# The second matmul of the first MoE: one float32 product in place of three rounded ones

## The chip, the core and the metric

The kernel runs on one core of a Trainium2 chip. The metric is the device time of one execution in microseconds; of the kernel before there are three runs, with a median of 643.16 us (642.65 to 646.45). One more execution was taken with the hardware profiler; every reading below is of that one. The engines are TensorE (PE, with its weight loads, PEld), VectorE (DVE), ScalarE (ACT), GpSimd (POOL) and SyncE (SP, which issues most of the DMAs).

## The reference

Three layers follow each other, all in float32 from outside:

```
# 1. state-space attention: 4 x 8 heads, 768 tokens, chunks of 32
y = (C B^T * decay) x + C state * decay          -> x of 3072 tokens x 256
# 2. first MoE (one dense expert)
h = x @ w_in            # 3072x256 @ 256x2048
g = h * cos(h)
x = g @ w_out           # 3072x2048 @ 2048x256
# 3. second MoE: 8 experts, the best one for each token, capacity 768
e = argmax(x @ w_gate); h = relu(x @ w1[e]); out = gate * (h @ w2[e])
```

The expert of a token is an argmax, so the first two layers are computed to nearly full float32.

## The kernel before

The 3072 tokens are six tiles of 512. For each tile the first MoE runs over 16 blocks f of 128 of the 2048 hidden features: 96 iterations, `it = 16 t + f`. One iteration is

- `mm1` (L919): six matmuls of 128x128 weights by 512 tokens into one PSUM bank `hp` (three banks rotate). Weights and tokens are split into a rounded high and a low part of the type F32R, and three of the four products are taken, for two halves of the 256 inputs;
- the cosine: `c_round` (ACT, L926), `c_frac` (DVE, L930), `c_sin` (ACT, L933), `c_mul` (DVE, L936), which leaves `g = h cos(h)` in float32 in a buffer `g` (three rotate) and frees `hp`;
- `c_hi`: the high part `gh` of g, by DVE (L947), or by ACT (L945) in the iterations 3 to 15 and 79 to 93; `c_lo`: the low part `gl = g - gh` by POOL (L952). Each has three buffers;
- `mm2` (L964): six matmuls of the type F32R, the products high x high, low x high and high x low for two halves of the 256 outputs, added up in two PSUM banks `yt` over the 16 blocks.

The weights come as 64-bit words of which the kernel puts together float32 numbers: `w_c1`, `w_c2`, `w_c3` (DVE, L879, L884, L889), once for each f, for w_in and w_out at a time (`wcv`, 512 columns). `w_hi` (ACT, L901) and `w_lo` (POOL, for some blocks DVE, L905) then split each half into its parts. This happens during the prologue and the first tile.

In the same stretches the other layers run: attention for the tiles that follow (`a_s`, L781; `a_m`, DVE L789, which multiplies scores in PSUM into `ex`; `a_y`, L835 and L839; `a_diff`, a POOL operation on 128x2048, L670), the routing of the tile before (`r_evac` to `r_store`, lines 970 to 1110; DVE L978 takes `yt` out of PSUM), and the conversion of the second MoE's weights (`w2_units`, DVE L1250). After the 96 iterations the second MoE works through 58 jobs of 128 tokens by half an expert (`b_mm1` L1606, `b_mm2` L1631, L1635). Its transposed activations `ht` use the buffers of `gh` and `gl` again, and its `hr` those of `g`.

The order on all engines is one list, written out by hand: every step is put at a position (its iteration number plus an offset from the table `OFF`, in iterations, with variants for the first tiles and the last one), the list is sorted, and each engine works off its own steps strictly in that order. So mm2 of iteration `it` is put at it + 4.08, behind mm1 of iteration it + 4:

```
for _, _, fn, a in sorted(work, key=lambda w: w[:2]):
    fn(*a)
```

Of the kernel before, what the change touches and what calls it, by code (L numbers as in the profile page):

```python
# [12 lines left out]
I32 = mybir.dt.int32
I64 = mybir.dt.int64
U32 = mybir.dt.uint32
AF = mybir.ActivationFunctionType
ALU = mybir.AluOpType
# [79 lines left out]
 'gh': 1.4743,
 'gh@0': 1.227,
 'gh@5': 1.853,
 'gl': 2.061,  # L100
 'gl@0': 1.372,
 'gl@5': 2.675,
# [249 lines left out]
 'woh': -2.85,
 'woh@2': -15.528,
 'woh@3': -5.859,
 'woh@4': -2.895,
 'wol': -2.362,
 'wol@2': -12.533,
 'wol@3': -3.479,
 'wol@4': -2.851,
# [15 lines left out]
def fused_kernel(ctx: ExitStack, tc: tile.TileContext, I, out: bass.AP):  # L375
    nc = tc.nc
    P = 128
    B, H, S = 4, 8, 768
    NTOK = B * S
    D = 256  # L380
    NCH = NTOK // P
    CPB = S // P
    T = 512
    NT = NTOK // T
    CT = T // P
    NF = 16
# [121 lines left out]
    C = {}  # L508
# [362 lines left out]
    WCV = {}  # L871

    def w_words(f):
        st = WST[f]
        return st.rearrange("p a b -> p (a b)").bitcast(I32).rearrange("p (a b) -> p a b", b=2)
# [9 lines left out]
                                       op0=ALU.logical_shift_right, op1=ALU.bitwise_or)  # L885

    def w_c3(f):
        a = WCV[f]
        nc.vector.scalar_tensor_tensor(a, w_words(f)[:, :, 1], -1073741824, a,  # L889
                                       op0=ALU.bitwise_and, op1=ALU.bitwise_or)  # L890
        WST.pop(f)

    def w_part(f, which, part):
        a = WCV[f].bitcast(F32)[:, which * D:(which + 1) * D]
        if which == 0:
            return a, w_in[:, f, part].rearrange("p k c -> p (k c)")
        return a, w_out[:, f, part, :]

    def w_hi(f, which):
        a, hi = w_part(f, which, 0)  # L900
        nc.scalar.activation(hi, a, AF.Copy)  # L901

    def w_lo(f, which, eng):
        a, hi = w_part(f, which, 0)
        eng.tensor_tensor(w_part(f, which, 1)[1], a, hi.bitcast(F32), op=ALU.subtract)  # L905
# [29 lines left out]
    def c_mul(it):  # L935
        nc.vector.tensor_tensor(GT[it], HP.pop(it), GT[it], op=ALU.mult)  # L936

    GHA = [[3, 16], [79, 94]]
    gh_act = lambda it: any(a <= it < b for a, b in GHA)

    def c_hi(it):
        gh = mq.tile([P, T], F32R, tag="gh", name="gh", bufs=3)
        GH[it] = gh
        if gh_act(it):
            nc.scalar.activation(gh, GT[it], AF.Copy)  # L945
        else:
            nc.vector.tensor_scalar(gh, GT[it], 1.0, None, op0=ALU.mult)  # L947

    def c_lo(it):
        gl = mq.tile([P, T], F32R, tag="gl", name="gl", bufs=3)  # L950
        GL[it] = gl
        nc.gpsimd.tensor_tensor(gl, GT.pop(it), GH[it].bitcast(F32), op=ALU.subtract)  # L952

    def mm2(it):
        t, f = divmod(it, NF)
        if f == 0:
            YT[t] = [ps.tile([P, T], F32, tag=f"yt{k}", name="yt") for k in range(2)]
        gh, gl = GH.pop(it), GL.pop(it)
        terms = [(j, k) for j in range(3) for k in range(2)]
        if f == NF - 1:  # L960
            terms.sort(key=lambda x: x[1])
        for j, k in terms:
            wl, g = ((0, gh), (1, gh), (0, gl))[j]
            nc.tensor.matmul(YT[t][k], w_out[:, f, wl, k * P:(k + 1) * P], g,  # L964
                             start=(f == 0 and j == 0), stop=(f == NF - 1 and j == 2))
# [302 lines left out]
    V, GP = nc.vector, nc.gpsimd  # L1268
    work = []

    def put(name, pos, fn, *a, t=None):
# [79 lines left out]
        (w_hi, 0, 0),
        (w_hi, 0, 1),
        (w_lo, 0, 0, GP),
        (w_lo, 0, 1, GP),
# [14 lines left out]
        (w_hi, 1, 0),
        (w_hi, 1, 1),  # L1370
        (w_lo, 1, 0, GP),
        (w_lo, 1, 1, GP),
# [9 lines left out]
        (a_st, 1, 1),  # L1382
    ]
    for n, (fn, *a) in enumerate(prologue):
        put(f'p{n}', .1 * n - 20, fn, *a)


    for it in range(NIT):
        t, f = divmod(it, NF)
        put('mm1', it, mm1, it, t=t)  # L1390
        put('rnd', it, c_round, it, t=t)
        put('frc', it, c_frac, it, t=t)
        put('sin', it, c_sin, it, t=t)
        put('mul', it, c_mul, it, t=t)
        put('gh', it, c_hi, it, t=t)
        put('gl', it, c_lo, it, t=t)
        put('mm2' if f else 'mm2f', it, mm2, it, t=t)
    for f in range(NF):
        if f > 3:
            put('wld', f, w_load, f, t=f)  # L1400
        for k, fn in enumerate((w_c1, w_c2, w_c3)):
            if f > 1:
                put(f'wc{k + 1}', f, fn, f, t=f)
        if f > 1:
            put('wih', f, w_hi, f, 0, t=f)
            put('woh', f, w_hi, f, 1, t=f)
            put('wil', f, w_lo, f, 0, GP, t=f)
            put('wol', f, w_lo, f, 1, V if f in [2, 11, 12, 13] else GP, t=f)
# [122 lines left out]
    part = lambda i: (0, i) if i < NE else (1, i - NE)  # L1531
    XK, XR, HT, YA = {}, {}, {}, {}
# [57 lines left out]
    HPB, HR, YP, SC = {}, {}, {}, {}  # L1590
# [211 lines left out]
```

## Time and profile before

| | us |
|---|---|
| three runs, median | 643.16 (642.65 to 646.45) |
| the profiled execution, its time | 644.14 |
| its span, first to last instruction | 642.4 |
| PE busy | 546.6 |
| DVE busy | 524.4 |
| POOL busy | 388.3 |
| ACT busy | 336.9 |
| mean granted TensorE clock | 0.932 of full speed |

The program is read in stages. Until about 33 us there is the prologue. From 33 to 105 us the iterations 0 to 11 run while the weights are put together; from there until about 446 us the remaining iterations run, with attention until about 366 us; after 453 us only routing, weights and the second MoE are left. A busy PE includes the time in which a matmul that stands alone drains, and matmuls at a lower clock take longer, so that a PE that is busy is not yet a PE at its peak. In the timeline, the distance between the starts of two rows is what a group of matmuls cost in the stream.

### The profile page before, as it was taken

To read this page: it belongs to the slowest core of one execution; us is meant where nothing else is said; L and a number is where in the kernel's file an instruction comes from. 1 tells how busy PE (TensorE), PEld (TensorE's weight loads), DVE (VectorE), ACT (ScalarE), POOL (GpSimd) and SP (SyncE) were. 2 spreads that over 40 slices of the span, in tenths; PEclk is the share of its full clock that TensorE was granted. 3 is DMA by queue.
4 is the path that set the end of the run, shared out by engine and by line. 5 is a ranking of instruction groups with operands and counts; after the bars stand their busy time and mean duration, and the time that the engine had idled before them with its cause. 6 is when DMAs were issued, how large, how long until landed. Compare 5 with 4: busy or idle time off the path is not lost. (4 is left out here: it accounts for less than half of the span.)

```text
span 642.4 us, 9919 instructions
## 1 busy us (share of the span) xinstructions
PE 546.6 (85%) x2860; PEld 381.8 (59%) x2860; DVE 524.4 (82%) x1009; ACT 336.9 (52%) x601; POOL 388.3 (60%) x409
## 2 busy tenths in 40 slices
PE   8848869998979897997989989685766799999993
PEld 7426647786767676785768777463433445555552
DVE  7989998779998999889987988988696885555663
ACT  5446677574547545473647658564735553333220
POOL 6889877766476756576665344478537563542343
PEclk9876898898999999898989999897978999999998
DMA  7799534250705162434431222045589989995772
GB/s 244 207 319 337 156 115 148 99 181 15 230 34 191 56 212 68 148 99 139 141 117 49 79 86 98 34 115 153 112 199 251 246 167 186 168 173 118 141 155 72
DMA packets 128021, 94.07 MB, mean 146 GB/s; under 512 B 81918, under 2 KB 116800, under 8 KB 127968
## 3 DMA queue, kind: packets, MB, share of 16 engines
q1 hardware_dynamic: 125184, 86.46, 50.2%
q0 software_dynamic: 2784, 6.97, 4.1%
q8 instruction: 26, 0.43, 0.3%
q14 instruction: 27, 0.22, 0.1%
HBM read 59.50 MB, written 15.54 MB: 117 GB/s over the span
## 5 line engine op out<-in xcount | busy, mean ns | idle before, releaser
L952 POOL TENSOR_TENSOR gl<-g,gh 128x512 fp32r<-128x512 f32 x96 | 131.5, 1370 | 82.2 <-DVE gh L947 54.6
L919 PE MATMUL hp<-xT,w_in 128*128 128x512 f32 x576 | 163.8, 424 | 6.6 <-DVE g L936 6.6
L919 PEld LDWEIGHTS hp<-xT,w_in 128*128 128x128 f32 x576 | 111.3, 202 | 32.1 <-DVE g L936 8.0
L964 PE MATMUL yt<-gh,w_out 128*128 128x512 f32 x384 | 109.8, 406 | 6.6 <-DVE gh L947 6.6
L933 ACT ACTIVATE g<-g,halfpi 128x512 f32<-128x512 f32 x96 | 69.2, 720 | 67.4 <-DVE g L930 65.0
L964 PEld LDWEIGHTS yt<-gh,w_out 128*128 128x128 f32 x384 | 75.7, 198 | 24.4 <-DVE gh L947 7.0
L1612 ACT ACTIVATE hr<-hp 128x512 f16<-128x512 f32 x58 | 34.5, 595 | 79.7 <-PE hp L1606 64.8
L936 DVE TENSOR_TENSOR g<-hp,g 128x512 f32<-128x512 f32 x96 | 65.6, 684 | 12.9 <-ACT g L933 12.5
L930 DVE SCALAR_TENSOR_TENSOR g<-g,hp 128x512 f32<-128x512 f32 x96 | 65.1, 678 | 10.0 <-ACT g L926 10.0
L1616 DVE SCALAR_TENSOR_TENSOR hr<-hp,hr 128x512 f16<-128x512 f32 x58 | 40.0, 689 | 34.8 <-ACT hr L1612 31.8
L964 PE MATMUL yt<-gl,w_out 128*128 128x512 f32 x192 | 61.9, 399 | 7.4 <-POOL gl L952 7.4
L926 ACT ACTIVATE g<-hp 128x512 f32<-128x512 f32 x96 | 56.0, 583 | 13.5 <-PE hp L919 11.6
L947 DVE TENSOR_SCALAR gh<-g 128x512 fp32r<-128x512 f32 x68 | 56.8, 836 | 0.0
L1631 PE MATMUL yp<-w2a,ht 128*128 x116 | 42.4, 402 | 15.1 <-DMA ht<-hr 8.2
L1631 PEld LDWEIGHTS <-ht 128*128 128x128 f16 x232 | 23.1, 100 | 44.4 <-DMA ht<-hr 16.9
L1643 POOL TENSOR_TENSOR sc<-gall,invb 128x1 f32<-128x1 f32 x58 | 13.1, 225 | 56.8 <-DVE yacc L1654 47.0
L1538 POOL DMA_INDIRECT xr<-xs_d,gat x29 | 36.0, 1240 | 18.3 <-DVE ob L1120 4.6
L964 PEld LDWEIGHTS yt<-gl,w_out 128*128 128x128 f32 x192 | 36.2, 192 | 17.9 <-POOL gl L952 10.3
L1631 PE MATMUL yp<-w2b,ht 128*128 x116 | 39.0, 379 | 0.0
L1659 POOL DMA_INDIRECT out_dram<-yacc,scat x29 | 29.0, 999 | 14.2 <-issue 14.2
L848 ACT ACTIVATE xT<-yp 128x256 fp32r<-128x256 f32 x24 | 9.2, 384 | 49.2 <-PE yp L839 49.1
L1606 PEld LDWEIGHTS <-xkeep 128*128 128x128 f16 x192 | 19.5, 104 | 25.2 <-issue 8.2
(239 smaller groups left out, 1126.0 us busy)
## 6 DMA issues: line engine op xcount, KB each, us to landing
wst<-in_w_dram SPq DMA_DIRECT2D x32, 512.0 KB
ex<-cumc_d SPq DMA_DIRECT2D x10, 1024.0 KB
pre<-in_w_io_dram SPq DMA_DIRECT2D x14, 512.0 KB
hl_d<-hl SPq DMA_DIRECT2D x10, 512.0 KB
b<-hl_d SPq DMA_DIRECT2D x40, 128.0 KB
c4s<-hl_d SPq DMA_DIRECT2D x40, 128.0 KB
xb<-in_xB_dram SPq DMA_DIRECT2D x11, 384.0 KB
xs_d<-xs SPq DMA_DIRECT2D x6, 514.0 KB
```

What stands on the lines that cost most here:

```text
L919: nc.tensor.matmul(hp, w_in[:, f, wl, k, :], xT[:, k, xl, :], start=(n == 0), stop=(n == 5))
L926: nc.scalar.activation(g, HP[it], AF.Copy, bias=MAGIC + 0.25)
L930: nc.vector.scalar_tensor_tensor(g, g, MAGIC, HP[it], op0=ALU.subtract, op1=ALU.subtract)
L933: nc.scalar.activation(GT[it], GT[it], AF.Sin, scale=SIN_SCALE, bias=halfpi)
L936: nc.vector.tensor_tensor(GT[it], HP.pop(it), GT[it], op=ALU.mult)
L947: nc.vector.tensor_scalar(gh, GT[it], 1.0, None, op0=ALU.mult)
L952: nc.gpsimd.tensor_tensor(gl, GT.pop(it), GH[it].bitcast(F32), op=ALU.subtract)
L964: nc.tensor.matmul(YT[t][k], w_out[:, f, wl, k * P:(k + 1) * P], g, start=(f == 0 and j == 0), stop=(f == NF - 1 and j == 2))
L1538: nc.gpsimd.indirect_dma_start(out=xr, out_offset=None, in_=xs_d, in_offset=bass.IndirectOffsetOnAxis(ap=gat[k][:, n:n + 1].bitcast(U32), ...
L1612: nc.scalar.activation(hr[:, 0], HPB[j], AF.Relu)
L1616: nc.vector.scalar_tensor_tensor(hr[:, 1], HPB.pop(j), 0.0, hr[:, 0], op0=ALU.max, op1=ALU.subtract)
L1631: nc.tensor.matmul(yp.rearrange("p a b -> p (a b)"), ht[:, k, :], w[:, bass.ds(e, 1), k].rearrange("p a l b -> p (a l b)"), start=(k == 0) ...
```

## The change

`mm2` takes `g` and `w_out` as they are, in float32: two matmuls (one for each half of the outputs) in place of six. So `c_hi`, `c_lo` and the buffers `gh` and `gl` of the first MoE fall away, w_out needs no `w_hi` and no `w_lo`, and it is one float32 array of half the size; `w_c3` is made in two halves, of which the one for w_out writes straight into `w_out`. `g` gets six buffers, since it now lives until mm2. mm2 moves one place forward (offset 4.08 to 3.1), and so does the evacuation of a tile's result (`rev`, 3.2 to 2.2). In the second MoE `ht` and `hr` share the six buffers `g`, except for every fourth `ht`, which stays in `gl`.

```
- 'mm2': 4.08,
+ 'mm2': 3.1,
- 'mm2@5': 3.549,
- 'mm2f': 4.008,
+ 'mm2@5': 3.1,
+ 'mm2f': 3.05,
- 'rev': 3.2003,
+ 'rev': 2.2003,
...
-    w_out = wpool.tile([P, NF, 2, D], F32R, tag="wB", name="w_out")
+    w_out = wpool.tile([P, NF, D], F32, tag="wB", name="w_out")
...
     def w_c3(f):
         a = WCV[f]
-        nc.vector.scalar_tensor_tensor(a, w_words(f)[:, :, 1], -1073741824, a,
-                                       op0=ALU.bitwise_and, op1=ALU.bitwise_or)
+        for which, dst in ((0, a[:, 0:D]), (1, w_out[:, f].bitcast(I32))):
+            c = slice(which * D, (which + 1) * D)
+            nc.vector.scalar_tensor_tensor(dst, w_words(f)[:, c, 1], -1073741824, a[:, c],
+                                           op0=ALU.bitwise_and, op1=ALU.bitwise_or)
...
-        g = mq.tile([P, T], F32, tag="g", name="g", bufs=3)
+        g = mq.tile([P, T], F32, tag="g", name="g", bufs=6)
...
-    def c_hi(it):
-        gh = mq.tile([P, T], F32R, tag="gh", name="gh", bufs=3)
-        GH[it] = gh
-        if gh_act(it):
-            nc.scalar.activation(gh, GT[it], AF.Copy)
-        else:
-            nc.vector.tensor_scalar(gh, GT[it], 1.0, None, op0=ALU.mult)
-
-    def c_lo(it):
-        gl = mq.tile([P, T], F32R, tag="gl", name="gl", bufs=3)
-        GL[it] = gl
-        nc.gpsimd.tensor_tensor(gl, GT.pop(it), GH[it].bitcast(F32), op=ALU.subtract)
...
-        for j, k in terms:
-            wl, g = ((0, gh), (1, gh), (0, gl))[j]
-            nc.tensor.matmul(YT[t][k], w_out[:, f, wl, k * P:(k + 1) * P], g,
-                             start=(f == 0 and j == 0), stop=(f == NF - 1 and j == 2))
+        g = GT.pop(it)
+        for k in range(2):
+            nc.tensor.matmul(YT[t][k], w_out[:, f, k * P:(k + 1) * P], g,
+                             start=(f == 0), stop=(f == NF - 1))
...
-        ht = HT[j] = mq.tile([P, 8, P], F16, tag="gh" if j % 4 else "gl", name="ht", bufs=3)
+        ht = HT[j] = mq.tile([P, 8, P], F16, name="ht",
+                                      **(dict(tag="g", bufs=6) if j % 4 else dict(tag="gl", bufs=3)))
```

What this does to the order, in three places. First DVE in the middle of the program, some of the iterations of the third and fourth tile; L936 (L922 in the changed kernel) is c_mul, L930 (L916) c_frac, L789 (L775) the a_m of attention. Before:

```order
L936 TENSOR_TENSOR g<-hp,g 128x512
L930 SCALAR_TENSOR_TENSOR g<-g,hp 128x512
L947 TENSOR_SCALAR gh<-g 128x512
L789 TENSOR_TENSOR ex<-sp,ex 128x2x2x128
L936 TENSOR_TENSOR g<-hp,g 128x512
L930 SCALAR_TENSOR_TENSOR g<-g,hp 128x512
L947 TENSOR_SCALAR gh<-g 128x512
L789 TENSOR_TENSOR ex<-sp,ex 128x2x2x128
```

Now:

```order
L922 TENSOR_TENSOR g<-hp,g 128x512
L916 SCALAR_TENSOR_TENSOR g<-g,hp 128x512
L775 TENSOR_TENSOR ex<-sp,ex 128x2x2x128
L922 TENSOR_TENSOR g<-hp,g 128x512
L916 SCALAR_TENSOR_TENSOR g<-g,hp 128x512
L775 TENSOR_TENSOR ex<-sp,ex 128x2x2x128
```

The copy to gh is gone between c_frac and the a_m that PE waits for; nothing else has moved here. Second, PE at the first iterations; L919 (L905) is mm1, L964 (L931) mm2, L800 (L786) and L781 (L767) attention. Before:

```order
L919 MATMUL hp<-xT,w_in 128x512 x18
L964 MATMUL yt<-gh,w_out 128x512 x4
L964 MATMUL yt<-gl,w_out 128x512 x2
L919 MATMUL hp<-xT,w_in 128x512 x6
L800 MATMUL up<-xb 128x256
L781 MATMUL sp<-c4s,b_456 128x256 x4
```

Now:

```order
L905 MATMUL hp<-xT,w_in 128x512 x18
L931 MATMUL yt<-g,w_out 128x512 x2
L905 MATMUL hp<-xT,w_in 128x512 x6
L786 MATMUL up<-xb 128x256
L767 MATMUL sp<-c4s,b_452 128x256 x4
```

Two matmuls stand where six stood, at the same place between the blocks of mm1. Third, PE at the end of the iterations, where the second MoE begins; L1595 (L1559) loads the experts' numbers into PE's registers, L1606 (L1570) is b_mm1 of the first job. Before:

```order
L964 MATMUL yt<-gh,w_out 128x512 x4
L964 MATMUL yt<-gl,w_out 128x512 x2
L1606 LDWEIGHTS xkeep
L1595 TENSOR_LOAD eblk_89
L1597 ISA x2
L1606 MATMUL hp_4140<-w1a,xkeep 128x512
```

Now:

```order
L931 MATMUL yt<-g,w_out 128x512 x4
L1559 TENSOR_LOAD eblk_89
L1561 ISA x2
L931 MATMUL yt<-g,w_out 128x512 x2
L1570 LDWEIGHTS xkeep
L1570 ISA
L1570 MATMUL hp_3368<-w1a,xkeep 128x512
```

Before, mm2 of the iterations 94 and 95 came behind the b_mm1 of job 0 and job 1; now mm2 of 94 comes ahead of job 0, and that of 95 ahead of job 1.

More of the change, by code (lines that the diff above doesn't have):

```diff
@@ L96 @@
  'gat@3': -0.318,
[L97 to L102, printed above, removed]
  'in0': 2.761,
@@ L117 @@
  'mm1': 0,
- 'mm2': 4.08,
+ 'mm2': 3.1,
  'mm2@0': 3.0557,
- 'mm2@5': 3.549,
- 'mm2f': 4.008,
+ 'mm2@5': 3.1,
+ 'mm2f': 3.05,
  'mm2f@0': 2.334,
- 'mm2f@5': 4.059,
+ 'mm2f@5': 3.05,
  'msk': -0.299,
@@ L240 @@
  'rc3@5': 3.817,
- 'rev': 3.2003,
- 'rev@4': 3.164,
- 'rev@5': 2.699,
+ 'rev': 2.2003,
+ 'rev@4': 2.2,
+ 'rev@5': 2.2,
  'rex': 11.998,
@@ L351 @@
  'wld@4': -7.281,
[L352 to L359, printed above, removed]
  'x': -0.704,
@@ L516, in cum_masks @@
         for n in ('lc', 'cc', 'ch'):
-            C[n] = mq.tile([96, 2, 4, 32], F32, tag="g", name=n, bufs=3)
+            C[n] = mq.tile([96, 2, 4, 32], F32, tag="g", name=n, bufs=6)
         C['of'] = mp.tile([96, 2, 2, 4], F32, tag="n2", name="of", bufs=2)
@@ L888, in w_c3, with w_part, w_hi, w_lo @@
         a = WCV[f]
-        nc.vector.scalar_tensor_tensor(a, w_words(f)[:, :, 1], -1073741824, a,
-                                       op0=ALU.bitwise_and, op1=ALU.bitwise_or)
+        for which, dst in ((0, a[:, 0:D]), (1, w_out[:, f].bitcast(I32))):
+            c = slice(which * D, (which + 1) * D)
+            nc.vector.scalar_tensor_tensor(dst, w_words(f)[:, c, 1], -1073741824, a[:, c],
+                                           op0=ALU.bitwise_and, op1=ALU.bitwise_or)
         WST.pop(f)
[L893 to L900, printed above, removed]
+    def w_part(f, part):
+        return WCV[f].bitcast(F32)[:, 0:D], w_in[:, f, part].rearrange("p k c -> p (k c)")
+    def w_hi(f):
+        a, hi = w_part(f, 0)
         nc.scalar.activation(hi, a, AF.Copy)
-    def w_lo(f, which, eng):
-        a, hi = w_part(f, which, 0)
-        eng.tensor_tensor(w_part(f, which, 1)[1], a, hi.bitcast(F32), op=ALU.subtract)
+    def w_lo(f, eng):
+        a, hi = w_part(f, 0)
+        eng.tensor_tensor(w_part(f, 1)[1], a, hi.bitcast(F32), op=ALU.subtract)
     NIT = NT * NF
-    HP, GT, GH, GL = {}, {}, {}, {}
+    HP, GT = {}, {}
     YT = {}
@@ L936, in c_mul @@
         nc.vector.tensor_tensor(GT[it], HP.pop(it), GT[it], op=ALU.mult)
-    GHA = [[3, 16], [79, 94]]
-    gh_act = lambda it: any(a <= it < b for a, b in GHA)
-    def c_hi(it):
-        gh = mq.tile([P, T], F32R, tag="gh", name="gh", bufs=3)
-        GH[it] = gh
-        if gh_act(it):
-            nc.scalar.activation(gh, GT[it], AF.Copy)
-        else:
-            nc.vector.tensor_scalar(gh, GT[it], 1.0, None, op0=ALU.mult)
-    def c_lo(it):
-        gl = mq.tile([P, T], F32R, tag="gl", name="gl", bufs=3)
-        GL[it] = gl
-        nc.gpsimd.tensor_tensor(gl, GT.pop(it), GH[it].bitcast(F32), op=ALU.subtract)
     def mm2(it):
@@ L957, in mm2 @@
             YT[t] = [ps.tile([P, T], F32, tag=f"yt{k}", name="yt") for k in range(2)]
[L958 to L961, printed above, removed]
-        for j, k in terms:
-            wl, g = ((0, gh), (1, gh), (0, gl))[j]
-            nc.tensor.matmul(YT[t][k], w_out[:, f, wl, k * P:(k + 1) * P], g,
-                             start=(f == 0 and j == 0), stop=(f == NF - 1 and j == 2))
+        g = GT.pop(it)
+        for k in range(2):
+            nc.tensor.matmul(YT[t][k], w_out[:, f, k * P:(k + 1) * P], g,
+                             start=(f == 0), stop=(f == NF - 1))
     R = {}
@@ L1350, in fused_kernel @@
         (a_evl, 0, 0),
[L1351 to L1354, printed above, removed]
+        (w_hi, 0),
+        (None,),
+        (w_lo, 0, GP),
+        (None,),
         (a_y, 0, 1),
@@ L1368, in fused_kernel @@
         (a_u, 1, 0),
[L1369 to L1372, printed above, removed]
+        (w_hi, 1),
+        (None,),
+        (w_lo, 1, GP),
+        (None,),
         (a_md, 1, 1, 0),
@@ L1384, in fused_kernel @@
     for n, (fn, *a) in enumerate(prologue):
-        put(f'p{n}', .1 * n - 20, fn, *a)
+        if fn:
+            put(f'p{n}', .1 * n - 20, fn, *a)
     for it in range(NIT):
@@ L1394, in fused_kernel @@
         put('mul', it, c_mul, it, t=t)
-        put('gh', it, c_hi, it, t=t)
-        put('gl', it, c_lo, it, t=t)
         put('mm2' if f else 'mm2f', it, mm2, it, t=t)
@@ L1404, in fused_kernel @@
         if f > 1:
[L1405 to L1408, printed above, removed]
+            put('wih', f, w_hi, f, t=f)
+            put('wil', f, w_lo, f, GP, t=f)
     put('c4z', 0, c4_zero)
@@ L1610, in b_relu @@
     def b_relu(j):
-        hr = HR[j] = mq.tile([P, 2, 512], F16, tag="g", name="hr", bufs=3)
+        hr = HR[j] = mq.tile([P, 2, 512], F16, tag="g", name="hr", bufs=6)
         nc.scalar.activation(hr[:, 0], HPB[j], AF.Relu)
```

## The prediction

> **What bounds the kernel now.** I read the page's 40 slices first, then the busy times by stage, then in each stage who waits for whom. In the slices PE and DVE are both high until about two thirds of the span, with the dips in turn:
>
> ```profile
> PE   8848869998979897997989989685766799999993
> DVE  7989998779998999889987988988696885555663
> ```
>
> The stages of the iterations (columns: length, then busy time of each engine with its instructions, the granted clock, the DMA's share and GB/s):
>
> ```profile
> core 0: us, PE busy (x) PEld busy (x) DVE busy (x) ACT busy (x) POOL busy (x), PEclk, DMA share, GB/s
> 33.00:105.00 72.00, 52.01 (x227) 38.51 (x227) 67.15 (x88) 42.37 (x73) 60.24 (x46) 0.79 0.65 213
> 105.00:120.00 15.00, 15.00 (x83) 12.07 (x82) 9.37 (x15) 13.17 (x18) 10.61 (x12) 1.00 0.67 222
> 120.00:380.00 260.00, 233.47 (x1247) 184.27 (x1246) 234.95 (x465) 145.74 (x243) 158.51 (x128) 0.95 0.34 111
> 380.00:400.00 20.00, 19.72 (x95) 16.11 (x94) 16.53 (x32) 17.89 (x38) 11.85 (x10) 1.00 0.38 123
> 400.00:420.00 20.00, 14.20 (x78) 10.78 (x76) 19.01 (x58) 10.29 (x17) 8.10 (x7) 0.83 0.13 43
> 420.00:446.00 26.00, 16.96 (x70) 12.31 (x69) 21.92 (x38) 16.73 (x26) 22.12 (x23) 0.94 0.49 136
> ```
>
> Where the weights are put together (33 to 105 us) DVE sets the pace, 67 of 72 us. At 105 and at 380 us it is PE, busy all the time. In the long middle, 120 to 380 us, both are busy nine tenths: PE stands idle for 26.5 us. The matmuls of mm2 in three stages count its iterations (six to one: 4.3, 62 and 6.8):
>
> ```profile
> 105.00:120.00 15.00, 6.47 (x26) 4.50 (x24) 1.00 0.67 222
> 120.00:380.00 260.00, 97.73 (x372) 72.37 (x372) 0.95 0.34 111
> 380.00:400.00 20.00, 10.39 (x41) 7.78 (x42) 1.00 0.38 123
> ```
>
> PE's waits in the middle, all for DVE:
>
> ```profile
> PE yp L835 <- DVE ex L789: 11.1, 6, 2.6
> PE yp L839 <- DVE ex L789: 8.5, 6, 2.6
> PE hp L919 <- DVE g L936: 6.2, 4, 1.9
> ```
>
> One of them in the timeline, first DVE, then PE:
>
> ```profile
> 253.47 3.62 DVE L947 TENSOR_SCALAR gh<-g 128x512 fp32r<-128x512 f32 x1
> 257.02 0.68 DVE L789 TENSOR_TENSOR ex<-sp,ex 128x512 f32<-128x512 f32 x1
> ```
>
> ```profile
> 257.75 0.49 PE L835 MATMUL yp<-bct,st 128*128 128x128 f32 x2 [2.22 <-DVE ex L789]
> ```
>
> The copy to gh held DVE for 3.62 us, the `ex` behind it came late, and PE lost 2.22 us. It is this copy that the change removes.
>
> **What mm2 costs on PE.** Before, from the start of its six matmuls to the start of what follows:
>
> ```profile
> 205.17 1.07 PE L964 MATMUL yt<-gh,w_out 128*128 128x512 f32 x4
> 206.07 0.61 PE L964 MATMUL yt<-gl,w_out 128*128 128x512 f32 x2
> 206.53 0.39 PE L992 MATMUL xp<-idwg,yT 128*128 128x136 f32 x2
> ```
>
> 206.53 - 205.17 = 1.36 us, 0.227 each. A plain float32 matmul of the same size exists in the prologue, the score matmuls of attention; the program has four of them with the tile bc, the trace eight records, so one is two records:
>
> ```profile
> L766 PE MATMUL spd<-pre,bc x8: 592/592/1193, 19.9 to 28.9; 128*128 128x512 f32 x8
> 27.63 1.88 PE L766 MATMUL spd<-pre,bc 128*128 128x512 f32 x4
> 29.35 0.38 PE L835 MATMUL yp<-bc,st 128*128 128x128 f32 x2
> ```
>
> Two of them back to back, with their weight loads, took 29.35 - 27.63 = 1.72 us, 0.43 a record. So mm2 will be two instructions, four records and 1.72 us: **0.36 us more per iteration**, fewer matmuls but more PE. The Trainium skill, FP8 and Floating Point Precision, section TensorE Precision Notes, speaks against the change here: it says that true float32 takes four passes through the array. Eight passes at the price of an F32R matmul would be 1.82 us, 0.46 more per iteration, and would add 7 us to the sum below (0.1 us in 73 iterations). The row is lower, and the row decides.
>
> **What goes from DVE and POOL.** The parts of g in the first two stages and the middle (columns as above, of the tile gh alone):
>
> ```profile
> 33.00:105.00 72.00, 13.76 (x44) 9.40 (x44) 2.84 (x3) 5.55 (x9) 17.25 (x11) 0.79 0.65 213
> 120.00:380.00 260.00, 69.81 (x248) 48.61 (x248) 52.51 (x63) 0.00 (x0) 82.07 (x62) 0.95 0.34 111
> ```
>
> In the middle DVE loses 52.5 of its 235 us (then 70% busy) and POOL 82 of 158.5. **PE alone is then the bound there.**
>
> The DVE rows of the weights, 33 to 105 us, and the shortest that such instructions get (min/median/max):
>
> ```profile
> L884 DVE SCALAR_TENSOR_TENSOR wcv<-pre,wcv 128x512 int32<-128x512 int32 x11 | 12.0, 1088 | 0.0
> L889 DVE SCALAR_TENSOR_TENSOR wcv<-pre,wcv 128x512 int32<-128x512 int32 x11 | 10.5, 956 | 0.1
> L879 DVE TENSOR_SCALAR wcv<-pre 128x512 int32<-128x512 int32 x10 | 6.9, 691 | 0.1
> L889 DVE SCALAR_TENSOR_TENSOR wcv<-wst,wcv 128x512 int32<-128x512 int32 x2 | 5.2, 2602 | 0.0
> L905 DVE TENSOR_TENSOR w_out<-wcv,w_out 128x256 fp32r<-128x256 f32 x3 | 2.5, 823 | 0.0
> L879 DVE TENSOR_SCALAR wcv<-pre x14: 410/482/1636, 9.1 to 98.7; 128x512 int32<-128x512 int32 x14
> L889 DVE SCALAR_TENSOR_TENSOR wcv<-pre,wcv x14: 676/1010/2271, 12.5 to 101.3; 128x512 int32<-128x512 int32 x14
> ```
>
> At their shortest the first four would take 11 x 0.68 + 11 x 0.68 + 10 x 0.41 + 2 x 0.68 = 20.4 us; they took 34.6. These 14 us come and go with what POOL does at the time: the same instruction takes 0.41 or 1.64 us. POOL's part goes down by 17.25 us (gl) and by nearly all of w_out's low parts:
>
> ```profile
> L905 POOL TENSOR_TENSOR w_out<-wcv,w_out 128x256 fp32r<-128x256 f32 x12 | 12.5, 1043 | 0.0
> ```
>
> Together 29 of 60 us, so half of the 14 should go: 7. The Trainium skill, SBUF — State Buffer, section Who interferes with whom, gives a mechanism: two engines share a pair of ports there, and the later one is blocked for a whole instruction; the 3.62 us copy agrees, and by the rule the w_c instructions stay exposed to the POOL work that is left, so that it would also give about a half.
>
> **The sum**, against the profiled 644.1 us (span 642.4; 1 us above the median of the runs):
>
> - 33 to 105 us: DVE loses 2.8 (gh), 2.5 (w_out low), 7 (less stretched), and gains something for w_c3 in two half instructions (between 0 and 13 times the 0.41 us of the shortest row above, 5.3; I take 1.5, since the columns stay the same and only the start is paid twice): 10.8 us. ACT and PE have room. Some of it will go to the weight DMAs, which become the next to be late. -8; bounds -3 (the two removals and half of them lost) and -13.
> - 105 to 120 us and 380 to 400 us: PE pays 0.36 in 4.3 and 6.8 iterations; it was full, nothing hides it. +3.9.
> - 120 to 380 us: PE pays 62 x 0.36 = +22; of its 26.5 us idle I let 5 stay, -21.5, because every wait of it is for DVE, which then has 30% to spare. Idle stretches also cost clock (0.95 here, 1.00 where PE is full: 5% of 260, 12 us of busy time); I let half come back, -6. Together -6. Bounds: no idle time and full clock, 22 - 26.5 - 12 = -17; half of the idle time and all of the lost clock stay, 22 - 13 = +9.
> - 400 to 446 us: ten iterations pay 3.7 us, but PE is idle for 15 of 46 us and waits there for gl and for DVE work (w2a) that POOL stretches. -3; bounds -8 and +3.
> - The end of the iterations. mm2 of 95 no longer stands behind that of 94 and the second job:
>
> ```profile
> 435.50 0.73 PE L964 MATMUL yt<-gl,w_out 128*128 128x512 f32 x2 [1.25 <-POOL gl L952]
> 446.26 2.72 PE L1606 MATMUL hp<-w1a,xkeep 128*128 x6 [4.65 <-DVE w2a L1250]
> 448.42 1.78 PE L964 MATMUL yt<-gh,w_out 128*128 128x512 f32 x4
> 450.50 1.47 PE L1606 MATMUL hp<-w1a,xkeep 128*128 x6
> 451.62 0.82 PE L964 MATMUL yt<-gh,w_out 128*128 128x512 f32 x2
> ```
>
> From 448.42 to 451.62 are 3.2 us by which the last routing can begin earlier after the wait of 4.65, part of which the second MoE's weight loads eat: -2; bounds -3 and 0.
>
> Moved steps: `rev` one place earlier makes ACT and DVE wait for the tile's last mm2, with c_frac of two iterations on behind it; PE has two mm2 and two mm1 (6 us) to do until it needs that. `ht` and `hr` in six common buffers are reused after three to four jobs, behind mm2 of a job that PE has done before the mm1 that the new one waits for: nothing.
>
> -8 + 3.9 - 6 - 3 - 2 = -15: **629 us**.
>
> **The rivals.** *Slower: PE's waits stay.* If the idle time of the middle comes from the fixed order (POOL's a_diff, ACT's exponentials ahead of `ex`, c_mul just in time with three banks hp) and not from DVE's load, PE pays 22 us there and gets nothing back; with +3.9, +3.7 and only -5 in the first stage that is +25: 669 us. For it: the `ex` rows are the end of a chain through POOL and ACT. Against it: the 3.62 us copy directly ahead of one. The point from which it decides: under 13 of the 38 us of idle time and clock come back, since the other terms make -9. A dearer float32 matmul, at the 0.592 us of a record that stands alone, would make 2.37 us of mm2 and belongs here; the pair in 1.72 us speaks against it.
>
> *Everything comes back*: all low bounds at once, 644 - 13 + 3.9 - 17 - 8 - 3 = 607 us. PE runs without a break after 520 us already, as the slices show, so it can; but attention's chains remain.
>
> *No change*: the middle breaks even (4 us of idle time stay and the clock stays at 0.95), the first stage gains 4, since its weight DMAs are late next (their share there is 0.65, the highest but one of the rows), and 105 and 380 us take that back: 644 us.
>
> **How the numbers follow.** Chances: the forecast 0.50, everything back 0.15, no change 0.20, slower 0.15. About 1% (6.4 us) is what a measurement of this kernel tells from no change. So faster 0.65, same 0.20, slower 0.15. The range: 611 to 650 us; the forecast's own bounds reach from 607 to 657, their ends only if all err to one side, and the slower rival stays outside.
>
> **What would show it.** Right: L931 with 384 records some 0.43 us apart; the stage of the middle with PE over 95% and the clock at 1.00, DVE near 70%; PE's waits for `ex` under 8 us; the w_c rows shorter; mm1 of iteration 15 some 8 us earlier. Wrong: more than 1.8 us for the pair of matmuls; PE still idle for over 15 us in the middle; the first stage as long as before with waits for DMA.

## The result, and the profile after

| | us |
|---|---|
| before, median of four runs | 644.31 (642.65 to 646.45) |
| after, median of four runs | 616.01 (613.48 to 616.82) |
| ratio, with its 95% interval | 0.9542 [0.9506, 0.9578] |
| the profiled execution after | 613.48, span 611.8, clock 0.967 |

The change makes the kernel 28 us faster (the profiled executions differ by 30.7). 15 were forecast. The 40 slices of the span after:

```profile
PE   8767979999999999999999999888568799999994
DVE  7989987657775878477756859875977865555663
PEclk9887999999999999999999999999878899999997
```

From the seventh slice to the 25th PE and its clock stand at 9; DVE, which stood at 7 to 9 there, goes down to between 4 and 8, but for the last of these slices.

For the accounting both programs are cut at the same iterations: at the start of mm1 of 0, 12, 16, 76 and 95, and at the end (columns as in the prediction: length, busy time of PE, PEld, DVE, ACT and POOL with their instructions, clock, DMA). Before:

```profile
32.90:96.60 63.70, 43.71 (x187) 32.48 (x187) 58.98 (x75) 37.12 (x62) 53.35 (x41) 0.80 0.71 231
96.60:112.70 16.10, 16.10 (x89) 12.10 (x88) 12.72 (x20) 12.02 (x19) 12.23 (x12) 0.85 0.48 154
112.70:360.60 247.90, 223.81 (x1191) 177.26 (x1190) 222.10 (x424) 141.47 (x235) 157.65 (x128) 0.95 0.35 115
360.60:436.10 75.50, 63.32 (x312) 49.15 (x312) 65.93 (x160) 51.08 (x93) 39.34 (x35) 0.95 0.29 89
436.10:643.00 206.90, 171.33 (x904) 90.88 (x902) 136.55 (x283) 78.08 (x144) 101.93 (x158) 0.94 0.80 166
```

After:

```profile
34.50:90.70 56.20, 43.73 (x167) 26.92 (x168) 53.43 (x84) 30.26 (x46) 26.81 (x23) 0.90 0.76 250
90.70:106.90 16.20, 16.20 (x79) 10.01 (x78) 11.82 (x20) 9.61 (x14) 6.56 (x7) 0.91 0.54 172
106.90:337.60 230.70, 230.70 (x1076) 147.75 (x1075) 158.73 (x373) 140.81 (x232) 75.75 (x65) 1.00 0.37 122
337.60:404.90 67.30, 64.68 (x268) 40.37 (x267) 53.29 (x145) 42.58 (x78) 15.17 (x19) 1.00 0.33 101
404.90:612.00 207.10, 173.59 (x897) 89.85 (x895) 132.42 (x283) 77.83 (x144) 94.85 (x152) 0.94 0.81 165
```

The differences by stage: start of the iterations +1.6, iterations 0 to 11 -7.5, 12 to 15 +0.1, 16 to 75 -17.2, 76 to 94 -8.2, the rest +0.6 (the last rows run past the ends of the spans, 642.4 and 611.8; inside them they are 206.3 and 206.9 us long). Since mm2 moved one place forward, the row of 16 to 75 holds 59 of them before and 60 after, and the next one 20 and 19; for the same work, at 1.36 us for one, these two differences are -18.6 and -6.8. All of these are differences of single executions, and the profiled one after is 2.5 us faster than its median, so one or two microseconds in a stage say little. Nearly the whole gain lies where DVE and POOL had been loaded, and none behind the iterations. In the middle row PE is busy for 230.70 of 230.70 us at a clock of 1.00. Before it had 24.1 us of idle time at 0.95.

The price of mm2 that the prediction took from the prologue holds. From the start of a pair to the start of what follows:

```profile
415.74 1.88 PE L931 MATMUL yt<-g,w_out 128*128 128x512 f32 x4
417.46 1.46 PE L1570 MATMUL hp<-w1a,xkeep 128*128 x6
```

417.46 - 415.74 = 1.72 us, four records, as forecast: 0.86 us for a matmul, 3.8 times the 0.227 us of an F32R matmul. The Trainium skill, FP8 and Floating Point Precision, section TensorE Precision Notes, gives four passes for a float32 matmul; this row fits it, with 0.215 us for each of eight passes. The 1.82 us worked out in the prediction came from taking the 0.227 us of an F32R matmul in the stream for a pass.

### The profile page after: what moved, and what is told of

It is laid out like the page before. It is cut to its first block, busy times and chain, and to the rows that moved or that the text cites. A ratio compares the mean times of both kernels' runs of the same rounds, so it can differ in the third digit from the quotient of the medians.

```text
span 611.8 us, 9092 instructions
## 1 busy us (share of the span) xinstructions
PE 557.4 (91%) x2668; PEld 334.5 (55%) x2668; DVE 439.3 (72%) x953; ACT 317.0 (52%) x557; POOL 241.3 (39%) x301
## 5 line engine op out<-in xcount | busy, mean ns | idle before, releaser
L931 PE MATMUL yt<-g,w_out 128*128 128x512 f32 x384 | 182.3, 598 | 7.3 <-DVE g L922 5.0
L905 PE MATMUL hp<-xT,w_in 128*128 128x512 f32 x576 | 166.6, 426 | 0.6 <-ACT xT L834 0.4
L905 PEld LDWEIGHTS hp<-xT,w_in 128*128 128x128 f32 x576 | 105.7, 192 | 36.1 <-issue 13.6
L931 PEld LDWEIGHTS yt<-g,w_out 128*128 128x128 f32 x384 | 72.7, 190 | 63.3 <-issue 46.6
L919 ACT ACTIVATE g<-g,halfpi 128x512 f32<-128x512 f32 x96 | 69.1, 719 | 60.0 <-DVE g L916 59.6
L922 DVE TENSOR_TENSOR g<-hp,g 128x512 f32<-128x512 f32 x96 | 65.8, 685 | 22.3 <-ACT g L919 21.6
L916 DVE SCALAR_TENSOR_TENSOR g<-g,hp 128x512 f32<-128x512 f32 x96 | 65.2, 679 | 16.3 <-ACT g L912 16.3
L1576 ACT ACTIVATE hr<-hp 128x512 f16<-128x512 f32 x58 | 34.5, 595 | 78.8 <-PE hp L1570 67.9
L1596 PE MATMUL yp<-w2a,ht 128*128 x116 | 42.9, 406 | 16.0 <-DMA ht<-hr 10.6
L1502 POOL DMA_INDIRECT xr<-xs_d,gat x29 | 35.5, 1224 | 30.3 <-DVE idn L1123 12.3
L1596 PEld LDWEIGHTS <-ht 128*128 128x128 f16 x232 | 23.3, 100 | 44.1 <-DMA ht<-hr 15.7
L995 POOL TENSOR_SCALAR xs<-x,n 128x256 f16<-128x256 f32 x24 | 11.2, 479 | 85.4 <-DVE rsm L986 41.7
L1596 PE MATMUL yp<-w2b,ht 128*128 x116 | 39.1, 379 | 0.0
L775 DVE TENSOR_TENSOR ex<-sp,ex 128x512 f32<-128x512 f32 x40 | 27.4, 686 | 14.0 <-PE sp L767 11.6
L1619 DVE SCALAR_TENSOR_TENSOR yacc<-yp,sc,yacc 128x256 f32<-128x256 f32 x58 | 27.9, 482 | 10.1 <-ACT yacc L1613 6.2
L656 POOL TENSOR_TENSOR ex<-ex,ncum 128x2048 f32<-128x2048 f32 x9 | 33.2, 3686 | 4.8 <-PE hp L905 3.9
L1600 PE MATMUL yp<-w2a,ht 128*128 x116 | 33.3, 287 | 0.0
L1600 PE MATMUL yp<-w2b,ht 128*128 x116 | 31.6, 273 | 0.0
```

The costliest lines, as they stand in the source:

```text
L656: eng.tensor_tensor(lt, lt, nn, op=ALU.add)
L905: nc.tensor.matmul(hp, w_in[:, f, wl, k, :], xT[:, k, xl, :], start=(n == 0), stop=(n == 5))
L916: nc.vector.scalar_tensor_tensor(g, g, MAGIC, HP[it], op0=ALU.subtract, op1=ALU.subtract)
L919: nc.scalar.activation(GT[it], GT[it], AF.Sin, scale=SIN_SCALE, bias=halfpi)
L931: nc.tensor.matmul(YT[t][k], w_out[:, f, k * P:(k + 1) * P], g, start=(f == 0), stop=(f == NF - 1))
L1502: nc.gpsimd.indirect_dma_start(out=xr, out_offset=None, in_=xs_d, in_offset=bass.IndirectOffsetOnAxis(ap=gat[k][:, n:n + 1].bitcast(U32), ...
```

## The experiments

Two theories stood against each other. By the first (**load**) the gain comes from the work that DVE and POOL lose, the copy gh and the subtraction gl, and PE's dearer mm2 fills gaps that are then gone. By the second (**places**) it comes from what was moved with it: mm2 and `rev` one iteration earlier, six buffers g, and the `ht` and `hr` of the second MoE in them. In the expectations the load stands as theory A (DVE's) and theory B (POOL's gl), the places as theory C. All kernels start from the changed one except the last. Their times by stage, from the profiled executions, cut at the same iterations:

| | 0 to 11 | 12 to 15 | 16 to 75 | 76 to 94 | median | ratio to before [95%] |
|---|---|---|---|---|---|---|
| before | 63.7 | 16.1 | 247.9 | 75.5 | 644.31 | |
| after | 56.2 | 16.2 | 230.7 | 67.3 | 616.01 | 0.9542 [0.9506, 0.9578] |
| 1 gh back | 56.8 | 15.4 | 235.2 | 68.2 | 622.65 | 0.9656 [0.9603, 0.9710] |
| 2 gl back | 58.8 | 15.7 | 231.5 | 71.0 | 628.83 | 0.9727 [0.9679, 0.9776] |
| 3 gh and gl back | 64.9 | 15.9 | 250.4 | 73.1 | 656.66 | 1.0153 [1.0092, 1.0214] |
| 4 six rounded matmuls | 56.3 | 15.3 | 211.0 | 64.8 | 590.30 | 0.9131 [0.9087, 0.9176] |
| 5 old places | 57.1 | 15.4 | 230.7 | 69.1 | 618.03 | 0.9555 [0.9512, 0.9598] |
| 6 ht and hr apart | 58.6 | 15.4 | 230.7 | 67.3 | 616.12 | 0.9522 [0.9472, 0.9572] |
| 7 before, gh on ACT | 63.9 | 16.0 | 231.5 | 77.9 | 633.22 | 0.9787 [0.9739, 0.9836] |

The runs before beside experiments 1 to 4 had a median of 645.71 us, beside 5 to 7 of 646.16.

### 1. The copy gh alone comes back

```
+    def c_hi(it):
+        gh = mq.tile([P, T], F32R, tag="gl", name="gh", bufs=3)
...
+            nc.vector.tensor_scalar(gh, GT[it], 1.0, None, op0=ALU.mult)
+        put('gh', it, c_hi, it, t=t)
```

> The changed kernel with the copy g to gh put back on DVE (ACT in the iterations 3 to 15 and 79 to 93), at its old place; nobody reads gh, and there is no gl. Nothing is left out of the result. PE's work is that of the changed kernel. Theory A (PE's idle time came from DVE's load, the copies above all): DVE gets 57 us back and PE idles again in the middle: 628 to 645 us. Theory B (it came from POOL's gl, as the last link of the chain to mm2 or through what POOL does to DVE's instructions): 614 to 621 us. Theory C (it came from mm2 and rev being put one place forward): 614 to 621 us.

The ratio is 0.0114 above that of the change; of 645 us these are about 7, not most of the gain. The median of 622.65 us lies between the ranges expected, below the 628 of theory A and just above the 621 of the others: the copy costs something, and far less than theory A in its plain form says. The middle, and the copies in the whole program:

```profile
105.10:340.30 235.20, 232.05 (x1076) 147.94 (x1075) 196.32 (x432) 141.84 (x235) 78.62 (x67) 1.00 0.38 121
L940 DVE TENSOR_SCALAR gh<-g x68: 411/420/3805, 42.6 to 414.4; 128x512 fp32r<-128x512 f32 x68
```

DVE is busy for 196 instead of 159 us there, one copy takes up to 3.8 us, and yet PE stands idle for only 3.2 us. The copy by itself does not make the waits of before.

### 2. The subtraction gl alone comes back

```
+    def c_lo(it):
+        gl = mq.tile([P, T], F32R, tag="gl", name="gl", bufs=3)
+        nc.gpsimd.tensor_tensor(gl, GT[it], GT[it], op=ALU.subtract)
+        put('gl', it, c_lo, it, t=t)
```

> The changed kernel with a POOL subtraction of the size of gl put back in every iteration (g minus g, read by nobody), and no copy to gh. Nothing is left out of the result. Theory A: POOL has room and DVE has few copies left that POOL can stretch, so 615 to 623 us, with 2 to 6 us of that in the stage where the weights are put together. Theory B, as far as it is POOL's load and not the chain: 628 us or more. Theory C: 614 to 621 us.

The subtraction here is a little lighter than that of before (POOL is busy for 143.51 us in the middle, before for 157.65). By the ratios about 12 us are gone (0.0185 of 645; the profiled execution, with 631.14 us the longest of its four, shows 17.7), but not in the middle (+0.8). That is the time of theory B, 628 us or more. The 12 us went in the first stage (+2.6, as theory A had it), in 76 to 94 (+3.7) and most of all behind them, where no theory had placed them: the rest takes 216.4 us to the end of the span instead of 206.9:

```profile
110.40:341.90 231.50, 231.19 (x1078) 147.79 (x1077) 170.07 (x373) 141.14 (x234) 143.51 (x128) 1.00 0.38 123
412.90:630.00 217.10, 177.14 (x896) 90.62 (x894) 135.90 (x283) 77.99 (x145) 100.22 (x160) 0.92 0.80 158
```

Where these 9.5 us begin stands in the timeline of this kernel, DVE first, then POOL, then PE and the row of the 3.7 us behind its wait (start, length; L1119 computes the experts' numbers that PE loads into its registers ahead of mm2 of 94):

```profile
414.34 1.68 DVE L1212 TENSOR_SCALAR inv<-inv 128x2 int32<-128x2 int32 x1
416.73 1.74 DVE L1641 TENSOR_SCALAR iv<-inv 128x8 f32<-128x8 f32 x1
421.86 1.52 DVE L1119 TENSOR_SCALAR ef<-ef 128x12 f32<-128x12 f32 x1
```

```profile
414.93 1.06 POOL L932 TENSOR_TENSOR gl<-g 128x512 fp32r<-128x512 f32 x1
417.38 1.06 POOL L932 TENSOR_TENSOR gl<-g 128x512 fp32r<-128x512 f32 x1
422.29 1.05 POOL L932 TENSOR_TENSOR gl<-g 128x512 fp32r<-128x512 f32 x1
```

```profile
425.17 3.77 PE L941 MATMUL yt<-g,w_out 128*128 128x512 f32 x4 [7.20 <-DVE w2a L1227]
```

```profile
425.10:428.80 3.70, 3.63 (x5) 1.38 (x6) 0.89 (x1) 0.00 (x0) 0.00 (x0) 0.50 0.69 209
```

In the changed kernel the third of these DVE instructions and the same matmul are:

```profile
410.71 0.17 DVE L1109 TENSOR_SCALAR ef<-ef 128x12 f32<-128x12 f32 x1
412.63 1.98 PE L931 MATMUL yt<-g,w_out 128*128 128x512 f32 x4 [2.27 <-DVE w2a L1217]
```

An instruction on twelve columns takes 1.52 instead of 0.17 us, and each of the three ends within 0.05 us of the end of a gl (421.86 + 1.52 = 423.38, 422.29 + 1.05 = 423.34). The three together lose 4.4 us. PE's wait grows by 4.9, from 2.27 to 7.20 us, and every job of the second MoE begins later. Behind the wait the granted clock is 0.50 (the row of 425.10 to 428.80), and the same mm2 takes 3.57 us (425.17 to 428.74) instead of 1.82 (412.63 to 414.45). The wait is put down to w2a, which stands right behind the step for the experts' numbers on DVE; mm2 begins 1.8 us after the end of that step in both kernels (423.38 to 425.17, 410.88 to 412.63). Whether PE waits there for the register load or for w2a was not tried by itself; either comes late by what DVE lost. The Trainium skill, SBUF — State Buffer, section Who interferes with whom, has the mechanism: the one fully blocks while the other holds the shared ports for an instruction. The ends agree. That the later one blocks does not show in the starts, since the records of DVE begin 0.4 to 0.7 us ahead of gl, during a DMA_INDIRECT of POOL. That is not what holds them: the eight small TENSOR_SCALAR of this run that met a DMA_INDIRECT alone took at most 0.17 us.

### 3. Both come back

```
+    def c_hi(it):
...
+    def c_lo(it):
+        nc.gpsimd.tensor_tensor(GH[it], GT[it], GH[it].bitcast(F32), op=ALU.subtract)
```

> The changed kernel with both put back, copy and subtraction, as before, but read by nobody, so that mm2 does not wait for them. Nothing is left out of the result. This is the float32 matmul alone, without what it saves on DVE and POOL. Theory A: the old idle time of PE plus 0.36 us in each iteration in which PE is not already waiting: 645 to 668 us, slower than the kernel before. Theory B by load: the same. Theory B by the chain (mm2 late because gl is late) and theory C: 616 to 635 us.

gl is made in the buffer of gh, since there is no room for both. This kernel takes 39 us more than the changed one by the ratios (0.0611 of 645), and 1.5% more than before. Its 656.66 us lie in the range of the load, 645 to 668, and far above the 635 to which the theories of the chain and of the places reach. 7 and 12 do not make 39: the two loads cost more together than apart. The first stage is back at 64.9 us (56.2 after, 56.8 and 58.8 with one of them), the middle at 250.4:

```profile
34.40:99.30 64.90, 46.72 (x168) 28.62 (x169) 62.59 (x86) 34.45 (x52) 41.10 (x33) 0.84 0.65 218
115.20:365.60 250.40, 237.45 (x1077) 150.40 (x1076) 221.51 (x431) 142.72 (x235) 158.85 (x128) 0.99 0.35 113
```

And the waits of before are there again (engine, what it waits for, us in total, times, longest):

```profile
PE yp L831 <- DVE ex L781: 8.2, 7, 1.7
PE yp L827 <- DVE ex L781: 5.4, 7, 1.5
```

DVE is busy for 170 of 231 us with gl, 196 of 235 with gh, 221.5 of 250 with both. The share alone does not say when `ex` comes late: experiment 7 has such waits at 79%. The timeline shows more. First the POOL operation that the kernel before has at the time of the copy in the prediction, then POOL, DVE and PE of experiment 3:

```profile
253.19 3.63 POOL L670 TENSOR_TENSOR ex<-ex,ncum 128x2048 f32<-128x2048 f32 x1
```

```profile
257.10 3.62 POOL L662 TENSOR_TENSOR ex<-ex,ncum 128x2048 f32<-128x2048 f32 x1
257.49 3.52 DVE L940 TENSOR_SCALAR gh<-g 128x512 fp32r<-128x512 f32 x1
261.66 0.49 PE L827 MATMUL yp<-bct,st 128*128 128x128 f32 x2 [1.46 <-DVE ex L781]
```

It is `a_diff`, not gl, that holds the copy for over 3 us, and the copy ends 0.3 us behind it. In both kernels this happens at all seven `a_diff` of the middle, each of which begins directly behind a gl, and the copy it holds is the one ahead of an `ex`. The seven waits of PE behind them are 15.9 of the 24.1 us of idle time before; in experiment 3 they are 6.4 of 13.0 us. Without gl, in experiment 1, `a_diff` begins at other times; it holds three copies for 3.8 us and three for 2.1 to 2.5, and PE does not wait behind any of them. So gl works here also by when it lets `a_diff` start. In the changed kernel the seven `a_diff` take as long, and the g and ex rows of DVE that meet them take 0.67 to 0.69 us, as elsewhere: the instruction that they held is gone. Of the 20 us by which the middle grows, 13 are idle time of PE and 7 longer busy time of the same matmuls.

This run also prices the slower rival: DVE and POOL loaded as before and the dearer mm2 on PE cost 250.4 against 247.9 us, 2.5 and not 22, because PE's extra work fills gaps that are there anyway: its idle time is 13.0 instead of 24.1 us, and the clock 0.99 instead of 0.95. (What makes it slower than before as a whole lies in the rest, 217.0 against 206.3 us, as in experiment 2.)

### 4. PE's price: six rounded matmuls, with nothing that makes the parts

```
-            nc.tensor.matmul(YT[t][k], w_out[:, f, k * P:(k + 1) * P], g,
-                             start=(f == 0), stop=(f == NF - 1))
+        for j in range(3):
+            for k in range(2):
+                nc.tensor.matmul(YT[t][k], w_out[:, f, k * P:(k + 1) * P], g,
+                                 start=(f == 0 and j == 0), stop=(f == NF - 1 and j == 2))
```

> The changed kernel with mm2 made of six F32R matmuls again, on a rounded g that c_mul writes straight and on the rounded w_out alone: the low parts of g and w_out are left out (the same rounded product is taken three times), so its time shows only what PE pays. If PE bounds the iterations at 0.36 us more for the float32 pair, this is faster than the changed kernel by 0.36 us in some 80 iterations, 29 us: about 587 us. If something else is close behind PE (DVE at 70 per cent, the chain of the cosine), it gains less: 595 to 608 us.

```profile
106.10:317.10 211.00, 209.89 (x1197) 170.03 (x1196) 163.26 (x371) 139.48 (x233) 78.58 (x66) 1.00 0.42 135
```

g and w_out are rounded to F32R as they are written, by DVE and by ACT, and `ht` and `hr` have buffers of their own, which experiment 6 shows to cost nothing. The 590.30 us are nearer to the 587 of PE alone as the bound than to the 595 of a second one close behind. Both middles keep PE full at a clock of 1.00, so the difference is the price: 230.7 - 211.0 = 19.7 us in 60 iterations, 0.33 each (0.36 forecast). In the middle the dearer matmul is paid in full; in the change it is the gaps of before that pay for it.

### 5 and 6. The moved steps and the shared buffers

Experiment 5 puts mm2 and `rev` back to their old places:

```
- 'mm2': 3.1,
+ 'mm2': 4.08,
...
- 'rev': 2.2003,
+ 'rev': 3.2003,
...
```

> The changed kernel with mm2 and rev at their old offsets (mm2 one place later, and behind the second MoE's first jobs at the end). Nothing is left out of the result. Theory C (the shorter pipeline is what gained): the stages of the iterations fall back by half or more, 628 us or above. Theory A (DVE's load): PE is full in the iterations either way, so they keep their length, and only the last routing comes later by some 3 us: 614 to 621 us.

Experiment 6 gives `ht` and `hr` buffers of their own, as before, and g of the iterations two sets of three:

```
-        ht = HT[j] = mq.tile([P, 8, P], F16, name="ht",
-                                       **(dict(tag="g", bufs=6) if j % 4 else dict(tag="gl", bufs=3)))
+        ht = HT[j] = mq.tile([P, 8, P], F16, tag="gh" if j % 4 else "gl", name="ht", bufs=3)
...
+        hr = HR[j] = mq.tile([P, 2, 512], F16, tag="g", name="hr", bufs=3)
```

> The changed kernel with ht and hr of the second MoE in separate buffers as before (three for hr, three for ht; g of the iterations takes turns between the two sets, six in all). Nothing is left out of the result. From the last routing's first matmul to the end the changed kernel takes 193.0 us, before 189.1. If the shared buffers cost that: 611 to 613 us with 189 to 190 us there. If that stretch waits for its weight loads, which do not come earlier: 614 to 618 us with 192 to 194 us there.

Both intervals overlap that of the change, and both middles are 230.7 us. With the old places the row of 16 to 75 holds 59 mm2 again and that of 76 to 94 holds 20, so the 1.8 us in the latter are the length of one mm2; over both rows together the old places cost these 1.8 us, and between the medians 2.0; theory A expected some 3, theory C over 12. The buffers cost nothing that can be measured: from the last routing to the end experiment 6 takes 193.8 us, the changed kernel 193.0. The theory of the places falls, except for those 2 us.

### 7. The kernel before with gh on ACT

The other way round: the six F32R matmuls and gl stay, and ACT makes gh in all iterations from 3 to 93.

```
-    GHA = [[3, 16], [79, 94]]
+    GHA = [[3, 94]]
```

> The kernel before with one change: the copy g to gh on ACT in all iterations from 3 to 93, so that DVE loses 63 copies (52 us in the middle) and PE keeps its six F32R matmuls. Nothing is left out of the result. Theory A in full (DVE's load was what held PE, and the float32 matmul is a price and no gain): DVE falls under 75 per cent in the middle, PE gets dense at 1.36 us per mm2, and it is faster than the changed kernel: 598 to 612 us. If POOL's gl or the longer chain through ACT, POOL and mm2 holds PE as well: 620 to 640 us. If ACT (142 us in the middle, plus 38) becomes the bound: 615 to 630 us.

13 of the 28 us come without any change of the matmuls, and they lie in the middle, where it reaches the time of the change, 231.5 us. The edit moves the copies of the iterations 16 to 78 alone, since ACT made those on either side already; so the first stage stays as it was, and 76 to 94 takes 2.4 us more. The middle is not dense here, PE has 13.5 us of idle time at a clock of 0.97, and it waits for `ex` although DVE is at 79% (182.10 of 231.60 us). The row of the middle, then PE's longest waits in it:

```profile
112.90:344.50 231.60, 218.08 (x1191) 173.15 (x1190) 182.10 (x372) 171.13 (x292) 160.75 (x128) 0.97 0.38 123
```

```profile
PE yp L839 <- DVE ex L789: 5.6, 4, 2.3
PE yp L835 <- DVE ex L789: 3.9, 2, 2.6
```

The 633.22 us fall into the range of 620 to 640, of which the expectation said that gl or the longer chain would hold PE; in the middle PE has no wait for gl, and what makes `ex` late there was not tried. So in the middle it is gh on DVE that counts while gl is there. What weighs at the two ends this run cannot say; experiments 1 and 2 give more of it to gl (+2.6 and +3.7 us) than to gh (+0.6 and +0.9). It also bounds what a mixture could bring: experiment 4's 211 us need the parts for nothing, and this kernel, which has ACT and POOL make them, is at 231.5 with mm2 at 1.36 us. No complete kernel here beats the change; a mixture of float32 and rounded blocks was not tried.

## Why the prediction was right in kind and half in size

- **What bounds it, and what mm2 costs on PE**: right. L931 has 384 records, the pair takes 1.72 us, and experiment 4 gives 0.33 us an iteration.
- **Iterations 0 to 11**, forecast -8, measured -7.5. The sum held, its terms did not. DVE's rows there after:

```profile
L878 DVE SCALAR_TENSOR_TENSOR wcv<-pre,wcv 128x256 int32<-128x256 int32 x10 | 9.5, 947 | 0.1
L870 DVE SCALAR_TENSOR_TENSOR wcv<-pre,wcv 128x512 int32<-128x512 int32 x10 | 7.2, 722 | 0.0
L878 DVE SCALAR_TENSOR_TENSOR w_out<-pre,wcv 128x256 int32<-128x256 int32 x10 | 5.9, 595 | 0.0
L865 DVE TENSOR_SCALAR wcv<-pre 128x512 int32<-128x512 int32 x9 | 5.6, 625 | 0.0
```

  w_c2 went from 1088 to 722 ns and w_c1 from 691 to 625: about 5 us of stretch came back, not 7. The two halves of w_c3 cost 947 + 595 instead of 956 ns, 5.9 us in ten, not 1.5. The split itself is not what costs: the median of a half is 0.41 us, but a few take up to 3.7, so it is stretch that came in at another place. DVE's busy time fell by 5.5 us and its idle time by 1.9 (4.7 to 2.8). So the forecast's 10.8 us of relief were 5.5, to which 1.9 of idle time came; that this stands so near the -8 is luck, since the cut from 10.8 to 8 was meant for weight DMAs. Of the signs named, w_c3 did not get shorter, and mm1 of iteration 15 begins 6.0 us earlier (109.9 to 103.9), not some 8.
- **12 to 15**, where PE is busy all the time: forecast +1.5 for mm2, because nothing would hide it, measured +0.1. The clock there went from 0.85 to 0.91, which the term did not have; the row that it rested on, from 105 to 120 us, had 1.00.
- **The start**: 1.6 us lost that no term had; the iterations begin at 34.5 instead of 32.9. PE's longest wait ahead of them is for the low part of w_in on POOL (before it was 2.5 us, for POOL as well; why it grew was not tried, and in experiments 1, 5 and 6 the iterations begin at 33.1, 34.2 and 35.5, so that one execution does not settle this term):

```profile
PE spd L752 <- POOL w_in L891: 3.8, 1, 3.8
```

- **The middle**: this is the step that failed in size. It let 5 us of idle time and half of the lost clock stay. PE pays 60 x 0.36 = 21.6 us, and 1.4 for the one mm2 that the row has more than before; idle time gives back 24.1, all of it; and busy time grew by only 6.9 (223.81 to 230.70), so 16.1 came back within it, where 6 were forecast and 12 were taken as all that there is. (With the 0.33 us of experiment 4 for the 0.36 it is 14.3.) The clock explains 12 of it: in the middle before, 23.9 us ran at 0.50, in six stretches, each of which begins less than 2 us behind one of the seven waits of experiment 3, and there were none after. The 2 to 4 us left are not taken apart here. 21.6 + 1.4 - 24.1 - 16.1 = -17.2, the step's own low bound of -17. The caution in it rested on the slower rival, that the order of the chain behind `ex` keeps the waits. It does not, though one link of that chain, `a_diff`, had a part in them by holding the copy (experiment 3): with DVE at 158.73 of 230.70 us (69%, 70% forecast) no wait for `ex` is left there. Here is one of the six stretches, behind the wait that the prediction shows at 257.75 us (the clock is the third number from the end), and then all waits for `ex` that the whole program has after:

```profile
258.40:261.60 3.20, 3.20 (x22) 2.06 (x15) 3.17 (x7) 0.99 (x2) 0.29 (x2) 0.50 0.00 0
```

```profile
PE sp L767 <- DVE ex L775: 0.5, 1, 0.5
PE yp L821 <- DVE ex L775: 0.2, 1, 0.2
```

- **76 to 94**: the second term that was too small. Forecast were +2.4 for mm2 and -3 between 400 and 446 us; measured -8.2. For the same number of mm2 it is -6.8 (see the accounting). PE's idle time there fell from 12.2 to 2.6 us, its waits for gl and half of one for the routing (`ob`) among it, and the clock rose from 0.95 to 1.00. DVE's weight steps lost a stretch of half a microsecond each. Before, two waits; after, what is left of the first; then the weight steps before and after:

```profile
PE pi L1130 <- DVE ob L1120: 4.9, 1, 4.9
PE yt L964 <- POOL gl L952: 3.8, 4, 1.5
```

```profile
PE pi L1097 <- DVE ob L1087: 2.3, 1, 2.3
```

```profile
L1250 DVE SCALAR_TENSOR_TENSOR w2a<-wst,wsc,w2a 128x1024 f16<-128x1024 f32 x6 | 10.3, 1752 | 0.0
```

```profile
L1217 DVE SCALAR_TENSOR_TENSOR w2a<-wst,wsc,w2a 128x1024 f16<-128x1024 f32 x6 | 7.4, 1276 | 0.0
```

- **The end**, forecast -2, measured +0.6. The step itself came: the last routing begins 34.6 us earlier, of which 3.4 lie behind the start of mm1 of 95 (17.25 us from there before, 13.85 after). Before and after:

```profile
453.35 0.50 PE L992 MATMUL xp<-idwg,yT 128*128 128x136 f32 x2
```

```profile
418.75 0.40 PE L959 MATMUL xp<-idwg,yT 128*128 128x136 f32 x2
```

  But the second MoE gives 4 us of it back: from there to the end of the span 193.0 (611.8 - 418.75) instead of 189.1 us (642.4 - 453.35). Its longest waits after are these; before, the first (L1631) was 8.2 us and the second (L1654) 2.1:

```profile
PE yp L1596 <- DMA ht<-hr: 10.6, 4, 3.9
PE yp L1596 <- DVE yacc L1619: 5.3, 2, 3.2
```

  Experiment 6 shows that the shared buffers are not the reason. Whether the weights' DMAs, issued at times that did not move along, hold it back was not tried and stays open.
- **The rivals**: the mechanism of the slower one falls twice, since the waits go when the copy and gl go (experiments 1 and 3) and since its +22 us would be 2.5 even where they stay. "Everything comes back" was right for the middle and for 76 to 94, wrong for the first stage and the end; 607 us were not reached, but the median of 616 is nearer to it than to the forecast of 629.

So the mechanism was right, DVE and POOL relieved and PE alone the bound of the iterations, and the two terms of idle time and clock were cut for a doubt that the profile did not bear out.

## What to carry to other kernels

Dearer work on the engine that seems the fullest can be had for nothing when its idle time comes from a second engine that the same change relieves; look at what each wait of the first is for before charging the price. Look one step further back too: what held the instruction that the wait is for? Here it was a copy, held by a third operation whose start a fourth one set. So do not price two loads one by one when they meet on one engine: each alone cost the middle little here (4.5 and 0.8 us), and the two together 19.7. The busy share of the second engine is a poor guide to it: at 83% PE idled for 3 us (experiment 1), at 79% for 13.5 (experiment 7). When the instruction that is held ahead of the waits falls away, let the forecast give all of the idle time back, and the clock with it; here both came.

## What the runs showed of the hardware that was not expected

- gh alone cost 7 us, gl alone 12, both 39 (DVE's busy share in the middle 83, 73 and 88%, 69% without).
- A DVE copy of 128x512 that met a POOL operation on 128x2048 (3.62 us) took 3.4 to 3.6 us instead of 0.42, seven times of seven before, while the g and ex rows of DVE took 0.67 to 0.69 us beside the same operation in the changed kernel.
- Three DVE instructions on 2 to 12 columns took 1.5 to 1.7 us instead of 0.17 while POOL worked on a 128x512 subtraction, ending with it. Steps that cost nothing on paper thereby moved PE's wait at the start of the second MoE from 2.3 to 7.2 us, and the matmuls behind the longer wait ran at a clock of 0.50.
- Behind six of the seven waits of PE for a held copy in the middle before, each of 1.3 to 2.7 us, the clock stood at 0.50 for 3.4 to 6.8 us.
- At a clock of 1.00 a float32 128x128x512 matmul takes 0.86 us in the stream, in two records of 0.43.
